# Later W1 regions asked for one by one, and the last block's gates by exponentials and a logarithm with their table loaded by name

## The chip, the cores and the metric

The kernel runs on one core of one Trainium2 chip. The metric is the device time of one execution in microseconds. The core has the engines TensorE (PE, with weight loads as PEld), VectorE (DVE), ScalarE (ACT), GpSimd (POOL) and SyncE (SP), each working through its own instructions in order. Transfers are issued by SP and by ACT in this kernel, and 16 DMA engines carry them out.

## What is computed

Three layers one after the other, all in float32 (cut from the reference):

```python
# attention with 128 random features, 4 batches x 8 heads, 576 positions, head size 64
kv = np.einsum('bhsm,bhsd->bhmd', phi(k), v);  z = np.sum(phi(k), axis=2)
x = (phi(q) @ kv) / (phi(q) . z + 1e-6)          # -> 2304 tokens x 512
# gated layer, 512 -> 1536 -> 512
gate = 1.0 / (1.0 + np.exp(-(x @ w_gate)))
x = gate * (x @ w_val) @ w_out
# soft mixture: 8 experts x 4 slots, F = 1024
logits = x @ phi
d = exp(logits - logits.max(0)); d /= d.sum(0) + 1e-9     # over the tokens
c = exp(logits - logits.max(1)); c /= c.sum(1) + 1e-9     # over the slots
slot_out[e] = np.maximum((d.T @ x)[e] @ w1[e], 0.0) @ w2[e]
return c @ slot_out
```

## The kernel before

All work is first recorded as jobs with a due time and then put into one order by `schedule()`, a list scheduler with costs of its own for each engine, which keeps a time from which an operation may start (`plan.floor`), a due time (`plan.t`) and the tables that ACT has loaded. The order is then issued by one helper line, so that all instructions carry the line L430, and rows are told apart by their tiles. Operations that two engines could do (casts, subtractions) are given to one of them by that scheduler.

The 2304 tokens lie in four blocks of 512 and a last one of 256 (`BLOCKS`). The gated layer walks over them in steps; a step f is one of 12 slices of 128 of the 1536 inner columns, and has three groups of matrix passes on TensorE: ga (x @ w_gate), va (x @ w_val) and o (the product with w_out of the step before). Every float32 operand is split into a rounded upper part and the rest, so that each product takes three passes (`three`); the upper part is a cast on ACT or DVE, the rest a subtraction on POOL or DVE (tiles w, ga_a, gt). Blocks 2 and 3 (`PAIR`) are done together by a scheme of seven products in `pair_jobs`, and the last stretch of it takes the down products of PAIR[0] and then of PAIR[1], twelve slices each. The last block of 256 tokens follows (steps `LAST` to `NS` - 1); then come the mixture's experts.

The weights pass through a ring of six tiles, ws, that SP loads from a scratch tensor wscr in DRAM (`load_part`, 512 KB for two slices or 256 KB for one). The last block's first weight, w0, comes by the first single 256 KB load.

When a block of 512 tokens has its x, the mixture's work on it (`moe2_chunks`) runs beside the next steps: the logits (`chunk_logits`, TensorE tiles `fl<-x2T,phs`), an exponential, four transposes on DVE (`x<-x2T`), and `chunk_back`, which writes the transposed halves back by sixteen moves of 64 KB (`x2T<-x`) on SP. `chunk_slot` uses them.

W1 has eight experts of four pieces of 0.5 MB, W2 as much again. `load_w1` asks for one expert in a region of SBUF that is free by then (`EXTAGS`: XT, XT, g2, g3, g4, XT, g0, g1, where g1 is two halves g1a and g1b) and issues four DMAs on ACT; in the trace they are `XT<-in_w`, `g<-in_w`, `g1a<-in_w` and `g1b<-in_w`. Six of the eight are asked for late, at due times of 32, 24, 16, 8 and 5 us before and 2 us after the planned start of the last block. Those are due times and not bounds: an operation of the stream "ex" may be issued 20 us early by the scheduler's lead. W2's pieces are issued on SP (`more<-in_w`, `gt<-in_w`, `ws<-in_w`). The DMA semaphores are eight, taken in turn by the transfers of SP and ACT together, and an issue waits until the transfer that used its semaphore before has landed.

The gate is a sigmoid. For the steps of blocks 0 and 1 it is exp(min(g, 0) - ln(1 + exp(-|g|))), with the product's PSUM tile ga kept until DVE has read it a second time; for the last block (`LAST <= i < SIGS`) it is one Sigmoid instruction on ACT. Exp and Ln are together in the table "natural_log_exp_and_others", and Sigmoid is in another one; ACT loads a table (ACT_TABLE_LOAD) whenever the next function isn't in the loaded one.

## Time and profile before

| | |
|---|---|
| three runs, us | 676.39, 667.46, 667.24 |
| median, us | 667.46 |
| profiled execution, us (its span) | 673.26 (671.5) |
| busy share of the span: PE, DVE, ACT, POOL | 96%, 74%, 62%, 41% |
| granted TensorE clock, mean | 0.989 |
| HBM traffic over the span | 199 GB/s |
| DMA packets moved | 138.48 MB |

The rows further down come from views of this one profiled execution. A timeline lists what an engine did in order, neighbours of one kind joined with their count; in brackets stands the idle time ahead of it and the instruction that ended it. The chain follows the work that ended last back from the end. Windows give busy time within a stretch. Names stand as output tile <- input tiles.

### The profile page before, as it was taken

The page shows a single profiled execution, that of the slowest core. Times are in us where ns is not written, and L with a number is a line of the kernel's source. Part 1 is how long each engine was busy: PE and PEld are TensorE (multiplying, and loading weights), DVE is VectorE, ACT ScalarE, POOL GpSimd, SP SyncE. Part 2 cuts the span into 40 slices and gives each one's busy share as a digit, 9 for nine tenths or more (in the row PEclk, how much of TensorE's full clock was granted, in tenths as well). Part 3 has the DMA queues.
Part 4 walks back from the last instruction along what each step waited for, and adds up shares of the span by engine and source line. Part 5 has one row for each costly group of instructions (what it writes and reads, how often), then busy time and mean ns, then how long its engine had stood idle before and what let it go on. Part 6 is the DMA issues. An engine that isn't in the chain of part 4 may idle for free.

```text
span 671.5 us, 12766 instructions
## 1 busy us (share of the span) xinstructions
PE 644.8 (96%) x4220; PEld 510.5 (76%) x4220; DVE 494.0 (74%) x1475; ACT 413.9 (62%) x938; POOL 273.9 (41%) x259
## 2 busy tenths in 40 slices
PE   7898999999999999899999999999999979999995
PEld 5675677778888778788877688788888859889564
DVE  5989998999899877779788986646638646756323
ACT  5899888889988867778776263443541326445012
POOL 0544445454544433326335645545542433342100
PEclk9999999999999999999999999999999989999898
DMA  7879566778886655623527442221239988777888
GB/s 250 307 267 300 203 216 211 258 231 282 279 274 228 175 180 190 196 84 111 165 74 248 158 124 68 74 82 32 67 100 331 297 260 303 232 234 266 310 341 243
DMA packets 63857, 138.48 MB, mean 206 GB/s; under 512 B 7216, under 2 KB 21296, under 8 KB 63792
## 3 DMA queue, kind: packets, MB, share of 16 engines
q1 hardware_dynamic: 57968, 120.30, 55.2%
q10 hardware_dynamic: 5824, 17.37, 7.6%
q8 instruction: 33, 0.54, 0.3%
q14 instruction: 32, 0.26, 0.1%
HBM read 116.15 MB, written 17.30 MB: 199 GB/s over the span
## 4 chain that ended last, share of the span: by engine, by line
PE 70%; DMA 10%; DVE 8%; ACT 3%; issue 3%; SPq 2%; POOL 2%; DVEq 0%; POOLq 0%; ACTq 0%
PE o L430 20%; PE fl L430 18%; PE ga L430 16%; PE va L430 16%; DVE g L430 3%; DMA g<-in_tok 3%; SPq L430 2%; DMA qscr<-g 2%; DMA ws<-wscr 1%; DMA g<-in_w 1%; DMA g<-qscr 1%; ACT ga_a L430 1%; DVE XT L430 1%; DVE x2T L430 1%; DMA XT<-in_w 1%
## 5 line engine op out<-in xcount | busy, mean ns | idle before, releaser
L430 POOL TENSOR_TENSOR w<-ws,w 128x512 fp32r<-128x512 f32 (+1 forms) x95 | 113.3, 1193 | 168.9 <-ACT w L430 54.4
L430 PE MATMUL o<-gt,w 128*128 128x512 f32 (+1 forms) x576 | 135.2, 374 | 2.4 <-ACT w L430 1.0
L430 PEld LDWEIGHTS o<-gt,w 128*128 128x128 f32 x576 | 97.9, 190 | 25.2 <-issue 4.1
L430 PE MATMUL ga<-XT,w 128*128 128x512 f32 (+1 forms) x432 | 100.9, 368 | 2.9 <-DVE XT L430 0.9
L430 ACT ACTIVATE w<-ws 128x512 fp32r<-128x512 f32 (+1 forms) x102 | 59.0, 581 | 71.4 <-PE o L430 24.2
L430 PE MATMUL va<-XT,w 128*128 128x512 f32 (+1 forms) x432 | 98.2, 363 | 0.0
L430 ACT ACTIVATE g<-g 128x128 f32<-128x128 f32 (+5 forms) x214 | 78.3, 422 | 17.7 <-DVE g L430 11.6
L430 PE MATMUL fl<-g,g 64*128 64x128 f32 (+4 forms) x686 | 84.3, 315 | 3.5 <-DVE g L430 1.5
L430 PEld LDWEIGHTS ga<-XT,w 128*128 128x128 f32 x432 | 69.9, 189 | 18.8 <-issue 3.0
L430 PEld LDWEIGHTS va<-XT,w 128*128 128x128 f32 x432 | 70.8, 189 | 12.9 <-issue 1.5
L430 PEld LDWEIGHTS fl<-g,g 64*128 64x128 f32 (+2 forms) x686 | 61.1, 185 | 24.0 <-issue 7.9
L430 ACT ACTIVATE x2T<-g 128x512 f32<-128x512 f32 x72 | 46.0, 667 | 5.3 <-DVE x L430 3.5
L430 ACT ACTIVATE g1b<-g1b,g 128x128 f32<-128x128 f32 x128 | 40.5, 389 | 1.2 <-DVE g L430 1.2
L430 PE MATMUL o<-gt,ga_a 128*128 128x512 f32 x144 | 37.2, 405 | 4.2 <-DVE gt L430 3.9
L430 DVE TENSOR_SCALAR x2T<-x2T 128x512 f32<-128x512 f32 (+1 forms) x72 | 36.4, 515 | 1.1 <-ACT x2T L430 1.0
L430 PEld LDWEIGHTS o<-gt,ga_a 128*128 128x128 f32 x144 | 27.3, 194 | 11.2 <-ACT ga_a L430 4.3
L430 DVE TENSOR_TENSOR w<-ws,w 128x512 fp32r<-128x512 f32 (+1 forms) x31 | 22.6, 731 | 17.3 <-ACT w L430 17.1
L430 DVE CUSTOM_DVE_ANT_0 g<-fl,g 128x128 f32<-128x128 f32 x142 | 32.2, 285 | 3.4 <-PE fl L430 3.3
L430 POOL TENSOR_TENSOR g<-g 128x512 f32<-128x512 f32 (+1 forms) x20 | 23.0, 1149 | 28.7 <-DMA g<-in_tok 19.5
L430 DVE TENSOR_TENSOR XT<-fl,XT 128x512 f32<-128x512 f32 x24 | 16.5, 689 | 21.9 <-PE fl L430 21.9
L430 ACT ACTIVATE ga_a<-ga_a 128x512 f32<-128x512 f32 x48 | 29.9, 623 | 3.7 <-DVE ga_a L430 3.4
L430 POOL TENSOR_TENSOR w<-x,w 128x512 fp32r<-128x512 f32 x17 | 21.8, 1284 | 25.3 <-ACT w L430 8.9
(261 smaller groups left out, 1262.9 us busy)
## 6 DMA issues: line engine op xcount, KB each, us to landing
ws<-wscr SPq DMA_DIRECT2D x42, 512.0 KB, 3.9
g<-in_wall SPq DMA_DIRECT2D x36, 512.0 KB, 4.9
ws<-wscr SPq DMA_DIRECT2D x54, 256.0 KB, 3.8
wscr<-x SPq DMA_DIRECT2D x36, 256.0 KB, 4.4
g<-in_qkT SPq DMA_DIRECT2D x15, 576.0 KB, 4.9
g<-in_tok SPq DMA_DIRECT2D x15, 576.0 KB, 5.3
g<-in_w ACTq DMA_DIRECT2D x16, 512.0 KB, 6.5
XT<-in_w ACTq DMA_DIRECT2D x12, 512.0 KB, 4.8
```

The lines of the kernel that those rows point to most:

```text
L430: ins = getattr(self.eng[e], method)(*a, **k)
```

## The change

There are five edits. `SIGS` goes from 99 to 0, so that the last block's twelve gates take the long form: Abs, Exp and Ln on ACT, a scalar_tensor_tensor on DVE that reads ga again, and an Exp on ACT, in the place of one Sigmoid. Ahead of PAIR[0]'s logits' exponential the common table is loaded by name (`preload_act_table_set`), and the scheduler counts it as loading that table. The six late W1 regions keep their due times (written as `W1AT`) but get floors in the planner's time of 480 to 535 (`W1FLOOR`). And `M2A` puts PAIR[0]'s mixture chunks 2 us later on the list.

```diff
--- before.py
+++ after.py
@@ -45,6 +45,7 @@
 
 W_LO = float(np.uint32(0x38000000).view(np.float32))
 BIG = 3.0e38
+EXP_LN = "natural_log_exp_and_others"
 W_HI = float(np.uint32(0x47EFFFFF).view(np.float32))
 
 
@@ -79,9 +80,11 @@
 SPANQ = 147.0
 SPAND = 33.0
 READY = 12.0
-SIGS = 99
+SIGS = 0
+W1AT = (1.0, 9.0, 17.0, 25.0, 28.0, 35.0)
+W1FLOOR = (480,491,502,513,524,535)
 EARLY = 30
-M2A = -32.0
+M2A = -30.0
 M2B = 0.66
 M2C = 3.75
 M2D = 0.7
@@ -399,6 +402,7 @@
                     alt = next(a for a in alts if a[0] == e)
                     c, held = self.cost(e, alt[1], alt[3], outs, ins)
                     want = {AF.Exp: 0, AF.Ln: 0, AF.Sigmoid: 1}.get(alt[3].get("func"), table) if e == "ACT" else table
+                    want = 0 if alt[1].startswith("preload") else want
                     if want != table:
                         c, table = c + RELOAD, want
                     if held:
@@ -1047,6 +1051,8 @@
             DVE.tensor_tensor(out=new, in0=new, in1=mrun[0:p], op=ALU.max)
         DVE.tensor_scalar(out=neg, in0=new, scalar1=-1.0, scalar2=None, op0=ALU.mult)
         DVE.tensor_copy(out=lt[0:p, 1, :], in_=ps)
+        if j == PAIR[0] and SIGS < NS:
+            plan.place([("ACT", "preload_act_table_set", (EXP_LN,), {})], [lt[0:p, 0, :]], [ps, SG[1]])
         ACT.activation(out=lt[0:p, 0, :], in_=ps, func=AF.Exp, bias=neg, accum_out=row)
         if j != DONE[0]:
             ACT.activation(out=old, in_=mrun[0:p], func=AF.Exp, bias=neg)
@@ -1133,13 +1139,15 @@
         t = T([128, 1024 * n], tag, F32, bufs)
         return [t[:, 1024 * c:1024 * c + 1024] for c in range(n)]
 
-    def load_w1():
+    def load_w1(k=None):
 
         e = len(W1)
+        plan.floor = 0.0 if k is None else W1FLOOR[k]
         if e < E:
             W1.append(pieces(EXTAGS[e], 3 if EXTAGS[e] == "XT" else 1))
             for c in range(4):
                 ACT.dma_start(out=W1[e][c], in_=w1[e, :, 1024 * c:1024 * c + 1024])
+        plan.floor = 0.0
 
     def load_w2():
 
@@ -1352,7 +1360,7 @@
                 plan.t -= 5.0 * last
 
     stream("att", T0)
-    ACT.preload_act_table_set("natural_log_exp_and_others")
+    ACT.preload_act_table_set(EXP_LN)
     DVE.memset(g4[:, 0:256], 0.0)
     warm(g4[:, 0:256], W0N, "va")
     for h in range(2):
@@ -1537,10 +1545,10 @@
             m2_jobs(0, start + 3.0, 60.0)
             jobs += [(start + 4.0, "ex", load_w1), (start + 12.0, "ex", load_w1)]
             start = pair_jobs(start)
-            jobs += [(start - SPAND + 1.0 + 8 * k, "ex", load_w1) for k in range(4)]
+            jobs += [(start - SPAND + x, "ex", lambda k=k: load_w1(k)) for k, x in enumerate(W1AT)]
             m2_jobs(PAIR[0], start + M2A, span * M2B)
             m2_jobs(PAIR[1], start + M2C, span * M2D)
-            jobs += [(start - 5.0, "ex", load_w1), (start + 2.0, "ex", load_w1), (start + 8.0, "ex", free_more),
+            jobs += [(start + 8.0, "ex", free_more),
                      (start + span * 0.9, "end", free_halves), (start + span * 0.85, "m2", join_slots)]
         for f in range(f0, f1):
             jobs += moe_jobs(i, start + span * (f - f0) / (f1 - f0), span / (f1 - f0))
```

The programs are the same up to the last down products of PAIR[0]. In full, ACT has 715 rows before and 745 after, DVE 1379 and 1386, PE 839 and 847, SP 247 and 248; table loads are 13 before and 5 after.

SP's order at PAIR[0]'s moves (`x2T<-x_588` before, `x_592` after; `ws<-wscr 128x2x512` is a 512 KB load, 128x512 a single one, of which the first is the last block's first weight). Before:

```order
L430 DMA ws<-wscr 128x2x512 x13
L430 DMA x2T<-x_588 32x512 x4
L430 DMA ws<-wscr 128x2x512
L430 DMA x2T<-x_588 32x512 x7
L430 DMA ws<-wscr 128x2x512
L430 DMA x2T<-x_588 32x512 x5
L430 DMA ws<-wscr 128x512 x9
```

and after:

```order
L434 DMA ws<-wscr 128x2x512 x12
L434 DMA x2T<-x_592 32x512 x2
L434 DMA ws<-wscr 128x2x512
L434 DMA x2T<-x_592 32x512 x7
L434 DMA ws<-wscr 128x2x512
L434 DMA x2T<-x_592 32x512 x7
L434 DMA ws<-wscr 128x2x512
L434 DMA ws<-wscr 128x512 x4
```

One 512 KB load has moved from ahead of the sixteen moves to behind the first two; the single loads follow the last of the three 512 KB loads.

DVE's order around the four transposes (`STREAM_TRANSPOSE`) that feed these moves. Before:

```order
L430 COPY x2T<-o_513 128x512
L430 COPY x2T<-o_515 128x512
L430 CAST ga_a<-ws 128x512
L430 CAST gt<-g_493 128x512
L430 TENSOR_TENSOR gt<-g_493,gt 128x512
L430 STREAM_TRANSPOSE x_588<-x2T 128x512
L430 CAST gt<-g_493 128x512
L430 STREAM_TRANSPOSE x_588<-x2T 128x512
L430 TENSOR_TENSOR gt<-g_493,gt 128x512
L430 TENSOR_REDUCE mx_582<-fl 128x1
L430 COPY lt<-fl 128x128
L430 TENSOR_TENSOR mx_582<-mx_582,mrun 128x1
```

and after:

```order
L434 CAST gt<-g_493 128x512
L434 CAST w_574<-ws 128x512
L434 TENSOR_TENSOR gt<-g_493,gt 128x512
L434 CAST gt<-g_493 128x512
L434 TENSOR_TENSOR gt<-g_493,gt 128x512
L434 STREAM_TRANSPOSE x_592<-x2T 128x512 x3
L434 CAST gt<-g_493 128x512
L434 STREAM_TRANSPOSE x_592<-x2T 128x512
L434 TENSOR_TENSOR gt<-g_493,gt 128x512
L434 TENSOR_REDUCE mx_587<-fl 128x1
L434 COPY lt<-fl 128x128
```

Two copies of x2T are no longer DVE's, and three transposes stand together, ahead of the logits' maximum (`TENSOR_REDUCE mx`).

ACT's order from PAIR[0]'s x2T copies up to the first single weights (`in_w` rows are W1 pieces of 0.5 MB). Before:

```order
L430 DMA g_598<-in_w 128x1024
L430 ACTIVATE w_589<-ws 128x512
L430 DMA g_609<-in_w 128x1024 x2
L430 ACTIVATE ga_a<-ws 128x512
L430 DMA g_609<-in_w 128x1024
L430 ACT_TABLE_LOAD
L430 ACTIVATE lt,mx_582<-fl,mx_582 128x128
L430 DMA g_609<-in_w 128x1024
L430 ACTIVATE mx_582<-mrun,mx_582 128x1
L430 ACTIVATE cs<-cs 128x128
L430 ACTIVATE ga_a<-ws 128x512
L430 DMA XT<-in_w 128x1024
```

and after:

```order
L434 DMA g_594<-in_w 128x1024 x2
L434 ACT_TABLE_LOAD
L434 ACTIVATE lt,mx_587<-fl,mx_587 128x128
L434 ACTIVATE mx_587<-mrun,mx_587 128x1
L434 DMA g_594<-in_w 128x1024
L434 ACTIVATE ga_a<-ws 128x512
L434 ACTIVATE cs<-cs 128x128
L434 DMA g_594<-in_w 128x1024
L434 ACTIVATE w_605<-ws 128x512
L434 DMA g_609<-in_w 128x1024 x2
L434 ACTIVATE w_611<-ws 128x512
L434 DMA g_609<-in_w 128x1024
```

The four x2T copies stand together on ACT just above this place after the change. By the row of the table load 13 W1 pieces have gone out before, counted from the first half of g1b, and 6 after. Between the last x2T copy on ACT and the last block's first weight (w_617 in both) stand 8 pieces before and 7 after.

ACT's order at the last block's first gates. Before:

```order
L430 ACT_TABLE_LOAD
L430 ACTIVATE ga_a<-ga 128x256
L430 ACTIVATE w_632<-ws 128x512
L430 DMA g_624<-in_w 128x1024
L430 ACTIVATE gt<-ga_a 128x256
L430 ACTIVATE ga_a<-ga 128x256
L430 ACTIVATE w_641<-ws 128x512
L430 DMA g1a<-in_w 128x1024
L430 ACTIVATE w_643<-ws 128x512
L430 ACTIVATE w_648<-ws 128x512
L430 ACTIVATE ga_a<-ga 128x256
```

and after:

```order
L434 ACTIVATE ga_a<-ga 128x256
L434 ACTIVATE ga_a<-ga_a 128x256
L434 ACTIVATE ga_a<-ga_a,one_b 128x256
L434 ACTIVATE w_632<-ws 128x512
L434 DMA XT<-in_w 128x1024
L434 ACTIVATE ga_a<-ga_a 128x256
L434 DMA XT<-in_w 128x1024
L434 ACTIVATE ga_a<-ga 128x256
L434 ACTIVATE w_641<-ws 128x512
L434 ACTIVATE ga_a<-ga_a 128x256
L434 ACTIVATE lt,mx_638<-fl,mx_638 128x128
L434 ACTIVATE ga_a<-ga_a,one_b 128x256
```

The table load and the Sigmoid (`ga_a<-ga`) of each gate have become Abs (`ga_a<-ga`), Exp (`ga_a<-ga_a`), Ln (`ga_a<-ga_a,one_b`) and Exp, with a weight cast or a W1 piece between them. Of the 24 late W1 pieces 3 stand behind the first gate before, and 10 after.

## Rows read from the trace of the kernel before

**Rows 1.** windows: busy us (instructions) of PE, PEld, DVE, ACT, POOL; PEclk, DMA share, GB/s
```profile
540.00:545.00 5.00, 1.07 (x5) 0.46 (x3) 1.70 (x4) 1.15 (x2) 0.56 (x1) 0.96 0.60 166
545.00:550.00 5.00, 4.72 (x16) 3.41 (x15) 4.13 (x6) 1.78 (x3) 2.54 (x3) 0.70 1.00 358
553.00:616.00 63.00, 60.60 (x500) 57.18 (x497) 41.23 (x89) 31.42 (x52) 26.06 (x20) 1.00 0.77 250
```

**Rows 2.** PE timeline of quiet steps: start, us, engine, operation, tiles, count
```profile
594.98 1.60 PE L430 MATMUL ga<-XT,w 128*128 128x256 f32 x12
...
599.30 1.60 PE L430 MATMUL ga<-XT,w 128*128 128x256 f32 x12
```

**Rows 3.** PE timeline around stall A, idle before and its releaser in brackets
```profile
537.63 2.88 PE L430 MATMUL o<-gt,w 128*128 128x512 f32 x12
544.44 1.49 PE L430 MATMUL o<-gt,ga_a 128*128 128x512 f32 x3 [3.92 <-DVE gt L430]
546.20 3.15 PE L430 MATMUL o<-gt,ga_a 128*128 128x512 f32 x9 [0.28 <-POOL ga_a L430]
549.19 1.07 PE L430 MATMUL o<-gt,w 128*128 128x512 f32 x4
```

**Rows 4.** chain that ended last: start, us, what
```profile
508.85 8.16 PE o L430 x36
...
537.87 4.71 DMA ws<-wscr
...
542.60 0.64 ACT w L430
...
543.26 0.69 DVE w L430
```

**Rows 5.** SP timeline: the x2T moves of block 0, then of PAIR[0]
```profile
391.63 2.41 SPq L430 DMA_DIRECT2D x2T<-x  x4
...
400.71 3.04 SPq L430 DMA_DIRECT2D x2T<-x  x5
...
522.17 4.22 SPq L430 DMA_DIRECT2D x2T<-x  x4
...
533.08 4.70 SPq L430 DMA_DIRECT2D x2T<-x  x5
```

**Rows 6.** DMA issues, KB each, median us to landing: 388 to 406, then 519 to 541
```profile
x2T<-x SPq DMA_DIRECT2D x16, 64.0 KB, 3.4
...
x2T<-x SPq DMA_DIRECT2D x16, 64.0 KB, 5.3
```

**Rows 7.** PE timeline around stall B
```profile
582.73 0.38 PE L430 MATMUL o<-gt,w 128*128 128x256 f32 x1 [0.97 <-ACT w L430]
583.79 1.57 PE L430 MATMUL o<-gt,w 128*128 128x256 f32 x11 [0.68 <-DVE gt L430]
...
589.37 1.46 PE L430 MATMUL o<-gt,w 128*128 128x256 f32 x10 [0.75 <-POOL w L430]
```

**Rows 8.** ACT timeline at stall B
```profile
582.05 0.63 ACT L430 ACTIVATE w<-ws 128x512 fp32r<-128x512 f32 x1 [5.40 <-DMA ws<-wscr]
```

**Rows 9.** ACT groups by form: total us, mean ns; table loads from 516 us on
```profile
L430 ACT ACT_TABLE_LOAD x9 | 11.5, 1283 | 0.2
L430 ACT ACTIVATE ga_a<-ga 128x256 f32<-128x256 f32 x12 | 4.6, 380 | 5.5 <-PE ga L430 5.4
...
L430 ACT ACTIVATE g<-g 128x256 f32<-128x256 f32 x1 | 0.4, 416 | 2.3 <-DMA g<-in_tok 2.3
...
L430 ACT ACTIVATE g<-fl,den_b 128x288 f32<-128x288 f32 x11 | 5.4, 488 | 1.0 <-PE fl L430 1.0
```

**Rows 10.** DVE groups by form, whole run
```profile
L430 DVE SCALAR_TENSOR_TENSOR ga_a<-ga,maske,ga_a 128x256 f32<-128x256 f32 x3 | 1.5, 485 | 3.7 <-PE ga L430 3.7
```

**Rows 11.** ACT timeline in the tail
```profile
618.72 1.28 ACT L430 ACT_TABLE_LOAD   x1
620.01 0.26 ACT L430 ACTIVATE dt<-dt 128x64 f32<-128x64 f32 x1
```

## Prediction

> **What bounds the kernel now.** I read the windows first, to see where TensorE is not full, then TensorE's timeline around each gap, and then the chain of work that ended last, backwards from the gap. In the windows of the stretch that the change touches, TensorE is short of work in two places [rows 1]: from 540 to 550 us it is busy for 1.07 and 4.72 of 5 us, with a granted clock of 0.70 in the second window, and from 553 to 616 it is busy for 60.60 of 63, the lack being around 582 to 590. Elsewhere the last block's steps run without a gap: a step is twelve passes each of ga, va and o, and from one step's ga to the next is 4.32 us, 1.44 for each twelve [rows 2].
>
> Stall A [rows 3]: the passes of f=8 start at 537.63, and twelve such passes take 2.72 us (a run of 36 took 8.16 [rows 4]), so f=9 could start at 540.35. It starts at 544.44: 4.09 us late. Its twelve passes then last until 549.19, 4.75 us instead of 2.72; 0.28 of this excess of 2.03 is a second wait, for POOL's ga_a, the rest is the lower clock. Together 6.1 us. The chain [rows 4] says what is late: the single ws load (512 columns, the first weight of the last block) was issued at 537.87, landed after 4.71 us, ACT cast it at 542.60, DVE subtracted at 543.26, and only then came the gt that TensorE waits for. ACT executes in order, so f=9's ga_a cast stood behind that first weight, and all of it behind one DMA. Why was it issued so late? The SP queue [rows 5]: sixteen x2T moves and two 512 KB ws loads stand ahead of it, from 522.17 to 537.78, 15.6 us. The same sixteen moves and two loads for block 0, when no W1 load is about, ran from 391.63 to 403.75, 12.1 us, and a move landed in 3.4 us instead of 5.3 [rows 6].
>
> Stall B [rows 7]: idle 0.97, 0.68 and 0.75 us at 582.73, 583.79 and 589.37, 2.4 us. ACT had waited 5.40 us for a ws load when it cast the weight that ended the first of them [rows 8]; PAIR[1]'s sixteen x2T moves sit between the ws loads on SP there.
>
> So 8.5 us can be won in this part of the program. The profiled execution is 671.5 us in span (673.26 in all), the median of three runs 667.46, 0.994 of the span; sums are made in the span and scaled by that.
>
> **The change, part by part.** *Table loads.* Nine from 516 us on become one (the named one ahead of the logits' Exp stands where the first of the nine is now): 8 x 1.283 = 10.3 us of ACT go [rows 9]. *Gates.* In each of twelve steps the Sigmoid (0.380) becomes an Abs of the same tile, taken at 0.38, and Exp, Ln and Exp, which the trace has for other widths: Exp on 128x256 in SBUF once at 0.416, Ln at 288 columns 0.488; so 0.42 + 0.49 + 0.42 = 1.33 us, x12 = 16.0 us. ACT gains 5.7 us net. DVE gains twelve scalar_tensor_tensor from PSUM at 0.485 = 5.8 us [rows 10]. The last block's 63 us have ACT at 31.4 and DVE at 41.2 us busy [rows 1], so both have room: about 37 and 47 of 63. Neither lies on TensorE's path as busy time; what counts is latency. The ga bank now comes free after Abs 0.38, one weight cast of 0.64 between [rows 4], Exp 0.42, Ln 0.49, DVE 0.49: 2.42 us after ga's last pass, and TensorE writes ga again 2.88 us after it (va and o, 1.44 each) [rows 2]. About 0.4 us to spare with the hand-offs still to pay. The gt of a step is wanted 5.76 us after ga's end (four passes of 1.44) and would be ready at about 4.3. Price nothing; cover gone (one ACT instruction held for over 0.4 us), each microsecond more is a microsecond on the end.
>
> *W1's loads.* 24 loads of 0.5 MB are issued by ACT from 500 us on. By the orders, 21 of them stand ahead of the last block's first gate now and 14 after the change; 3 and 10 behind it. Between the last x2T copy on ACT and the first weight of the last block, the stretch of stall A, 8 stand now and 7 after: barely lighter. What is lighter is the backlog before it.
>
> *SP.* One 512 KB ws load moves behind the first two moves, so the single ws load now has sixteen moves and three loads ahead of it. DVE has two x2T copies less, and does three of the four transposes together, ahead of the logits' reductions that stood between them. The first move is issued at 522.17 now, and I put it 2.3 us earlier, at about 519.8; this is my estimate from the order (two copies and three reduction rows fewer ahead of the last transpose), with no row for it. From there the single ws goes out after 12.1 + 0.6 us at best (block 0's rate) and 15.6 + 0.6 at worst: 532.5 to 536.0. It lands 4.71 us later, and f=9 starts 1.86 us behind that, as now (542.58 to 544.44): 539.1 to 542.6, against 540.35 needed. So the wait of 4.09 becomes 0 to 2.2. With seven W1 loads still in the stretch I go nearer the worst: start at 541.8, wait 1.5, 2.6 won. Of the 2.03 behind it I take half, 1.0, as the pause before it is shorter. Bounds of stall A: 1.9 to 6.1 won, taken 3.6.
>
> *Stall B.* PAIR[1]'s moves should start some 2 us earlier with the rest, which could spare all 2.4 us; but seven more W1 loads now run among the last block's ws loads, which could cost the same again at other steps. Bounds 2.4 won and 2.4 lost (more is the second rival); I take 0.4 won.
>
> *The rest.* M2A's 2 us move the logits between TensorE passes that have no gap: nothing. One table load less in the tail, at 618.72 [rows 11], could bring its own 1.28 us at most; taken as nothing, since TensorE has passes of its own there. Weight casts that change from ACT to DVE: nothing, as both have idle time in the stretch.
>
> Sum: 671.5 − 3.6 − 0.4 = 667.5, times 0.994 = 663.5 us.
>
> On the table loads the Trainium skill, page "ScalarE: Activation LUTs", section "What ACT_TABLE_LOAD costs", counts 1283 ns and a drain of about 1380 ns for each switch; by that the eight loads would be 21.3 us of ACT and ACT would gain no busy time but lose 5. Here a load is 1.28 us and the next activation starts right behind it [rows 11], so the drain isn't seen, and the sum goes by 10.3.
>
> **The rivals.**
> 1. *Both stalls go whole.* If the moves run at block 0's rate, A costs nothing, and the last block's W1 loads fit: −8.5, 663.0 in span, 659. For it: the best bound 539.1 is ahead of 540.35. Against: seven W1 loads stay in the stretch, and B has its own cause.
> 2. *The W1 loads on ACT hold the gates: slower.* Ten loads now stand in ACT's order between gate instructions. The DMA semaphores are shared by ACT and SP in turn, and an issue waits when the transfer eight before it hasn't landed: between 522 and 538 such waits stretched SP's sixteen moves by 3.5 us [rows 5]. If each of the seven added loads holds ACT by 1.5 us, that is 1.1 over the spare 0.4, x7 = 7.7; less the 2.6 to 3.6 won at A, +4 to +5: 675.5 in span, 672. It decides from about 0.9 us held a load on. For it: the DMA engines' share is already 0.77 over the last block [rows 1], and ACT idled 5.40 us for one ws load there [rows 8]. Against: the seven are spread over some 40 us, and ACT had 31.6 of 63 us free.
> 3. *Stall A isn't W1's.* If the sixteen moves take 15.6 us at whatever load, and the ws that now stands behind them takes 4.71 or more, A shrinks by the 1.7 us of the earlier start and B grows by as much: within 1 us of 667.5 in the median.
>
> A rule of the Trainium skill speaks for the second rival: page "DMA: Bandwidth & Descriptors", section "Issuing engines are not separate DMA queues": transfers of all issuing engines share the 16 DMA engines and interleave. By it nothing is relieved where W1's seven loads stay beside the moves, and the last block's ws loads pay for the other seven. The trace agrees that they share: a move landed in 3.4 us without W1's loads and in 5.3 with them [rows 6].
>
> **How the numbers follow.** The likeliest, 0.45: both shortened, 661 to 666, predicted 663.5. Both gone 0.15 (659). Stall A not W1's 0.15 (667). Slower 0.25 (669 to 674). The range, 657 to 673, reaches 2 us below the first rival, since the shorter runs without a profile may not have the stalls at the profile's size, and to the second's price with a little over it; it leaves out some two in ten, at both ends. What a measurement of this kernel can tell from no change is about 2%, 13.3 us: faster than 654.1 would need more than the 8.5 us that can be won, 0.03; slower than 680.8 would need rival 2 at twice its price, 0.05; within, 0.92.
>
> **What would show it.** Right: TensorE's idle before f=9 (the o passes on gt and ga_a) under 2.2 us; the single ws load issued before 536; the clock in the window behind it above 0.70; table loads from 516 us on down to one; ACT's busy share of the last block about 37 of 63 us. Wrong: TensorE waiting on a ga pass for DVE or on an o pass for a gt in steps 1 to 8 of the last block, with ACT idle before it for a DMA; f=9 starting later than 544.4; or ws loads of the last block landing after more than 6 us.

## The result and the profile after

The changed kernel is slower. Over twenty runs each, its median is 674.86 us (670.55 to 679.74) and that of the kernel before 669.62 us; the ratio is 1.0077, with a 95% interval of 1.0055 to 1.0099. The prediction was 663.5 us with a range up to 673.0: the wrong side, and outside the range. It was made against a median of three runs of 667.46 us; twenty runs put the kernel before 2.2 us higher, but as a ratio the forecast was 0.994, so that doesn't rescue it. Medians and ratios, here and below, leave out runs more than 1.5% above the fastest of the same kernel (one of six in e4, one of ten in e8, three of twelve in e12, none elsewhere). A ratio is the one on record, over runs of the same session, and not the quotient of the two medians shown.

| | before | after |
|---|---|---|
| median of 20 runs, us | 669.62 | 674.86 |
| span of the profiled execution, us | 671.5 | 674.6 |
| mean granted clock of TensorE | 0.989 | 0.985 |
| ACT busy in the last block | 31.42 of 63.00 us | 36.69 of 69.90 us |
| table loads in the whole program | 13 | 5 |

TensorE's timeline of the kernel after, first around the old stall A and then in the last block; the columns are start, duration, operation, tiles and count, and in brackets the idle time ahead and what ended it:

```profile
540.67 0.47 PE L434 MATMUL o<-gt,ga_a 128*128 128x512 f32 x1 [3.16 <-DVE gt L434]
541.52 0.79 PE L434 MATMUL o<-gt,ga_a 128*128 128x512 f32 x2 [0.37 <-DVE gt L434]
542.98 4.21 PE L434 MATMUL o<-gt,ga_a 128*128 128x512 f32 x9 [0.67 <-POOL ga_a L434]
546.98 3.36 PE L434 MATMUL o<-gt,w 128*128 128x512 f32 x10
```

```profile
578.42 1.70 PE L434 MATMUL ga<-XT,w 128*128 128x256 f32 x12 [1.05 <-DVE ga_a L434]
...
588.44 2.93 PE L434 MATMUL ga<-XT,w 128*128 128x256 f32 x12 [3.75 <-DVE ga_a L434]
591.17 2.52 PE L434 MATMUL va<-XT,w 128*128 128x256 f32 x12
...
606.48 1.70 PE L434 MATMUL va<-XT,w 128*128 128x256 f32 x12 [0.87 <-DVE ga_a L434]
...
620.05 1.66 PE L434 MATMUL o<-gt,w 128*128 128x256 f32 x12 [0.75 <-DVE gt L434]
```

Stall A is still there: idle 3.16, 0.37 and 0.67 us, 4.20 in all, exactly the sum of [rows 3]. The two groups behind it, starting at 540.67 and 546.98, then take 6.31 us (with the two shorter waits) and 3.75 us, where the kernel before took 4.75 and 2.81 and a group without a stall takes 2.72. Where the kernel before waited in the last block for weights, 2.4 us in all [rows 7], the kernel after waits at ga and va for DVE's ga_a, the gate: 1.05, 3.75 and 0.87 us, and 0.75 for a gt at its end; with 0.30 for a weight that is 6.7 us. Behind the longest of these a group of twelve passes takes 2.73 us (588.44 to 591.17) instead of 1.44.

Windows of the kernel after, for the stretches that answer to [rows 1] (columns as there):

```profile
540.00:545.00 5.00, 3.28 (x8) 2.12 (x9) 4.07 (x7) 0.51 (x1) 2.08 (x2) 0.71 0.90 274
545.00:550.00 5.00, 5.00 (x16) 3.91 (x15) 1.63 (x3) 0.63 (x1) 0.48 (x1) 0.61 0.77 227
551.70:621.60 69.90, 62.94 (x502) 59.34 (x498) 41.18 (x100) 36.69 (x83) 28.13 (x21) 0.95 0.79 262
585.00:590.00 5.00, 1.56 (x7) 1.56 (x8) 2.94 (x11) 0.71 (x2) 2.29 (x2) 0.64 1.02 393
590.00:595.00 5.00, 5.00 (x32) 5.00 (x32) 1.56 (x6) 2.65 (x6) 1.28 (x1) 0.67 0.66 240
```

The lower clock lasts two windows after stall A (0.71, 0.61) where it lasted one before (0.70), and the kernel before has no such window in the last block, where this one has two (0.64, 0.67). Part of that is chance: a second profile of the kernel before (e5, further down) has 0.50 and 0.94 after stall A, and one window of 0.68 in the last block.

Profiles of two executions can't be laid over each other by their times: the kernel after reaches the same point of the program 3.7 us earlier, and the second profile of the kernel before reaches it 4.4 us earlier, by chance of what lies ahead. A point behind which the orders begin to differ is the group of twelve o passes that starts at 511.40 us before and at 507.69 after. Measured from there, the kernel after is later by 0.0 us at the start of f=9, 2.5 at the first gate, 3.7 at the ga of step 5, 8.2 at that of step 8, 8.9 at the first passes of the tail (`ga<-x2T,phs`), and 6.8 at the end. So 2.5 us are lost around stall A, 6.5 in the last block (69.9 us from its first gate to the tail, 63.4 before), and 2.1 come back in the tail. Of the 6.5 us, 4.3 are more idle time of TensorE (6.7 for 2.4); the rest is mostly the passes at the lower clock.

Why the last block loses: ACT and DVE of the kernel after around its longest stall, and the chain of work that ended last there.

```profile
576.43 0.63 ACT L434 ACTIVATE w<-ws 128x512 fp32r<-128x512 f32 x1 [1.52 <-DMA ws<-wscr]
...
579.71 0.33 ACTq L434 DMA_DIRECT2D g<-in_w  x1
...
580.34 0.33 ACTq L434 DMA_DIRECT2D g<-in_w  x1
...
580.73 0.43 ACTq L434 DMA_DIRECT2D g1a<-in_w  x1
...
588.42 0.42 ACT L434 ACTIVATE ga_a<-ga_a 128x256 f32<-128x256 f32 x1 [6.46 <-DVE ga_a L434]
```

```profile
583.67 0.43 DVE L434 CAST w<-ws 128x512 fp32r<-128x512 f32 x1 [3.34 <-DMA ws<-wscr]
...
586.97 0.43 DVE L434 CAST w<-ws 128x512 fp32r<-128x512 f32 x1 [2.07 <-DMA ws<-wscr]
...
587.97 0.42 DVE L434 SCALAR_TENSOR_TENSOR ga_a<-ga,ga_a 128x256 f32<-128x256 f32 x1
```

```profile
580.07 6.77 DMA ws<-wscr
...
588.05 0.34 DVE ga_a L434
...
588.44 2.93 PE ga L434 x12
```

The gate's Exp at 588.42 waits 6.46 us for DVE; DVE's second reading of ga at 587.97 stands behind two weight casts that wait 3.34 and 2.07 us for their ws loads; and the chain names the ws load, issued at 580.07 and landing after 6.77 us. Three W1 pieces of 0.5 MB were issued beside it, at 579.71, 580.34 and 580.73, SP had put a W2 piece ahead of it at 579.17, and the window behind them (585 to 590) moves 393 GB/s. So this stall has two parts, a late ws load and a gate that stands behind it in an in-order queue. The experiments take them apart.

### The profile page after: what moved, and what is told of

Its sections match the earlier page's. It is cut to its first block, busy times and chain, and to the rows that moved or that the text cites. A ratio compares the mean times of both kernels' runs of the same rounds, so it can differ in the third digit from the quotient of the medians.

```text
span 674.6 us, 12781 instructions
## 1 busy us (share of the span) xinstructions
PE 644.3 (96%) x4220; PEld 511.6 (76%) x4220; DVE 490.6 (73%) x1485; ACT 416.8 (62%) x967; POOL 273.9 (41%) x260
## 4 chain that ended last, share of the span: by engine, by line
PE 70%; DMA 11%; DVE 9%; ACT 4%; issue 2%; SPq 2%; POOL 1%; DVEq 0%; POOLq 0%; ACTq 0%
PE o L434 20%; PE fl L434 19%; PE ga L434 16%; PE va L434 16%; DMA ws<-wscr 4%; DVE g L434 4%; DMA g<-in_tok 2%; DMA qscr<-g 2%; SPq L434 2%; ACT ga_a L434 1%; DMA g<-qscr 1%; DMA x2T<-x 1%; DVE ga_a L434 1%; DMA g<-in_w 1%; DVE x2T L434 1%
## 5 line engine op out<-in xcount | busy, mean ns | idle before, releaser
L434 POOL TENSOR_TENSOR w<-ws,w 128x512 fp32r<-128x512 f32 (+1 forms) x96 | 115.3, 1202 | 177.0 <-ACT w L434 48.1
L434 ACT ACTIVATE g<-g 128x128 f32<-128x128 f32 (+5 forms) x214 | 78.1, 422 | 15.4 <-DVE g L434 10.6
L434 ACT ACTIVATE ga_a<-ga_a 128x512 f32<-128x512 f32 (+1 forms) x72 | 39.7, 552 | 12.3 <-DVE ga_a L434 11.9
L434 ACT ACTIVATE ga_a<-ga 128x512 f32<-128x512 f32 (+1 forms) x36 | 18.8, 522 | 21.7 <-PE ga L434 21.5
```

The source lines that it names most:

```text
L434: ins = getattr(self.eng[e], method)(*a, **k)
```

## The experiments

Each kernel is the kernel before or after with the edit shown. Two readings are given: the ratio to the kernel before, and, from the profile, by how much it is later (+) or earlier (−) than the kernel before, counted from the common point. Step 5 and step 8 are the ga of that step, and can be off by about 1 us, since passes of the mixture stand ahead of them in one order and behind them in another; "tail" is the first pass behind the last block, where all of them are through.

| us, minus before | f=9 | first gate | step 5 | step 8 | tail | end | ratio |
|---|---|---|---|---|---|---|---|
| before, second profile (e5) | −0.6 | 0.7 | 0.7 | 2.2 | 2.2 | 2.2 | 1 |
| after | 0.0 | 2.5 | 3.7 | 8.2 | 8.9 | 6.8 | 1.0077 |
| gates only (e1) | 5.7 | 3.9 | 6.3 | 4.0 | 4.2 | 2.0 | 1.0033 |
| floors only (e2) | 0.6 | 1.6 | 2.1 | 6.7 | 8.2 | 6.4 | 1.0096 |
| after without floors (e3) | 0.9 | 2.2 | 5.0 | 1.5 | 1.7 | −0.5 | 1.0033 |
| after, gate that reads ga once (e4) | −1.8 | −0.4 | 0.6 | 7.9 | 10.6 | 8.4 | 1.0178 |
| after, W1 to a quarter (e6) | −3.4 | −4.9 | −4.9 | −4.6 | −5.4 | −7.1 | 0.9914 |
| before, W1 to a quarter (e7) | −4.1 | −5.0 | −5.0 | −6.9 | −6.9 | −8.5 | 0.986 |
| floors only, W1 to a quarter (e13) | −3.5 | −5.0 | −4.6 | −7.0 | −5.7 | −7.4 | 0.9874 |
| before, join_slots earlier (e9) | 1.7 | 1.7 | 1.7 | 0.4 | 0.4 | −1.3 | 1.0009 |
| after, last floors later (e10) | −1.6 | −0.1 | −0.5 | −1.4 | 2.1 | −0.1 | 1.0025 |
| both held back (e14) | −3.9 | −3.4 | −3.4 | −1.0 | 0.9 | −1.0 | 0.9969 |
| the same with Sigmoid (e15) | −4.1 | −3.2 | −3.7 | −3.1 | −0.9 | −0.9 | 1.0017 |

The second profile of the kernel before shows how far two executions of one program differ by themselves: 2.2 us at the end. Single runs of it, told by their whole times, differ by up to 10 us (666.45 to 676.39), so that a difference of 2 us between two profiles shows nothing by itself.

### Gates or floors: e1, e2, e3

e1 is the kernel after with M2A and the six W1 regions as before:

```diff
-M2A = -30.0
+M2A = -32.0
...
-            jobs += [(start - SPAND + x, "ex", lambda k=k: load_w1(k)) for k, x in enumerate(W1AT)]
+            jobs += [(start - SPAND + 1.0 + 8 * k, "ex", load_w1) for k in range(4)]
...
-            jobs += [(start + 8.0, "ex", free_more),
+            jobs += [(start - 5.0, "ex", load_w1), (start + 2.0, "ex", load_w1), (start + 8.0, "ex", free_more),
```

> Of the change only the gates and the table loaded by name; the six W1 regions and M2A as before. Theory A (the long gate is the cause: its Exp and the scalar_tensor_tensor that frees ga stand behind weight casts that wait for a ws load, and TensorE waits at ga): slower than before by 2 to 5 us, ratio 1.003 to 1.0075, with idle time of TensorE at ga passes ended by DVE's ga_a of over 2 us. Theory B (the W1 pieces moved into the last block make its ws loads late, and the gates cost nothing by themselves): within 1 us of before, ratio 0.9985 to 1.0015, and no idle time at ga passes.

Measured: 671.98 us, ratio 1.0033 (1.0010 to 1.0055). TensorE's timeline of it:

```profile
539.72 0.79 PE L434 MATMUL o<-gt,w 128*128 128x512 f32 x1 [6.10 <-DVE gt L434]
541.18 4.63 PE L434 MATMUL o<-gt,w 128*128 128x512 f32 x10 [0.67 <-POOL w L434]
...
580.18 1.69 PE L434 MATMUL ga<-XT,w 128*128 128x256 f32 x12 [1.95 <-DVE ga_a L434]
```

Theory A's size and sign hold at their lower edge, and a wait of 1.95 us at a ga pass for DVE's ga_a is there (0.39 at another). But the profile is later than before by 3.9 us at the first gate already, where no long gate has run yet, because stall A came out larger (6.10 and 0.67 us idle); the last block itself, where the gates run, takes 63.7 us, against 63.4 and 64.9 in the two profiles of the kernel before. So the slowdown of e1 is not seen where theory A has it.

e2 keeps the floors alone:

```diff
-SIGS = 0
+SIGS = 99
...
-M2A = -30.0
+M2A = -32.0
```

> Of the change only the floors of the six W1 regions; Sigmoid gates and M2A as before. Theory A: within 1.5 us of before, ratio 0.997 to 1.002, since a Sigmoid frees ga in one instruction. Theory B: slower by 3 to 5 us, ratio 1.0045 to 1.0075, TensorE waiting in the last block for weights (o passes ended by ACT or POOL w).

Measured: 677.11 us, ratio 1.0096 (1.0063 to 1.0129): theory B's sign, and more than its size. TensorE's longest wait in the last block and the piece of the chain ahead of it:

```profile
582.13 0.80 PE L434 MATMUL va<-XT,w 128*128 128x256 f32 x2 [3.83 <-ACT w L434]
```

```profile
573.88 7.46 DMA ws<-wscr
```

The Sigmoid kernel waits too, and as long (3.83 us): here for the weight itself, whose ws load took 7.46 us. So floors alone give the whole slowdown, as far as two overlapping intervals tell, and the gates don't add to it: the last block takes 69.95 us here and 69.90 in the kernel after. Both kernels wait for a late ws load; with the long gate the gate stands behind the weight cast and TensorE stops at ga, with the Sigmoid it stops at the pass that needs the weight.

e3 is the kernel after with the regions asked for as before, so e1 with M2A at −30:

```diff
-            jobs += [(start - SPAND + x, "ex", lambda k=k: load_w1(k)) for k, x in enumerate(W1AT)]
+            jobs += [(start - SPAND + 1.0 + 8 * k, "ex", load_w1) for k in range(4)]
...
-            jobs += [(start + 8.0, "ex", free_more),
+            jobs += [(start - 5.0, "ex", load_w1), (start + 2.0, "ex", load_w1), (start + 8.0, "ex", free_more),
```

> The changed kernel with the six W1 regions asked for as before; gates and M2A stay changed. Theory A: slower than before by 2 to 5 us, like the gates alone. Theory B: within 1 us of before. If M2A is a cause of its own, this run stands apart from the gates alone by over 2 us.

Measured: 671.88 us, ratio 1.0033 (1.0007 to 1.0058), as e1: M2A is no cause of its own. Its last block takes 62.9 us, no more than before. By the ratios of the three runs, the floors cost about 6.4 us alone, the gates and their table about 2.2 (the interval of e1 runs from 0.7 to 3.7), and together they cost 5.2.

### A gate that reads ga once: e4

```diff
+        if i >= LAST:
+            ACT.activation(out=a, in_=ps, func=AF.Exp, scale=-1.0)
+            DVE.tensor_scalar(out=a, in0=a, scalar1=1.0, scalar2=None, op0=ALU.add)
+            DVE.reciprocal(out=a, in_=a)
+            return a
```

> The changed kernel, but the last block's gate is 1/(1+exp(-ga)): one Exp on ACT that reads ga once, then an addition of 1 and a reciprocal on DVE in SBUF, with the same table. ga is free after one ACT instruction, as with the Sigmoid. Theory A: 4 to 7 us faster than the changed kernel, at or below before (ratio 0.993 to 1.001), no idle time over 0.5 us at ga passes. Theory B: 0 to 2 us faster than the changed kernel, ratio 1.005 to 1.008, as the ws loads are as late as before.

Measured: 682.33 us, ratio 1.0178 (1.0149 to 1.0207), slower than either theory allowed. A reciprocal of 128x256 is dear, and twelve of them put 20.9 us on DVE; but DVE is busy for 53.6 of the 74.5 us of the last block, and TensorE's longest wait there is another one:

```profile
L434 DVE RECIPROCAL ga_a<-ga_a 128x256 f32<-128x256 f32 x12 | 20.9, 1742 | 0.1
```

```profile
584.19 1.89 PE L434 MATMUL fl<-x2T,dt 128*32 128x512 f32 x2 [5.93 <-DMA ws<-wscr]
```

TensorE waits 5.93 us for a transfer, ahead of passes of the mixture that read what the sixteen x2T moves bring; the profile names a ws load, and the last of these moves landed at 583.74 us. It is between steps 5 and 8 that this kernel loses 7.3 us. Its waits for the gate's ga_a come to 0.4 us in all, as theory A expected of a gate that frees ga at once, and the time that theory A promised for that isn't won. So the run speaks for late transfers. How much of the slowdown is the reciprocal's own isn't shown.

### The kernel before a second time: e5

> The kernel before, unchanged, for a second profile of it. If stall A (4.2 us of idle time at f=9), stall B (2.4 us) and the lower clock from 620 to 630 us belong to its order, all three are seen again, each within 1 us (clock 0.81 and 0.85, within 0.05); what is not seen again is chance of one execution, and a difference between two profiles of that size says nothing.

Stall A (3.30 us) and B (3.21) are there again, each within the 1 us that was expected; B is 0.8 us longer and at one place instead of three. A lower clock in the tail is there again too, but not at its size: 0.66 and 1.00 in the two windows, for 0.81 and 0.85.

```profile
539.43 5.97 PE L430 MATMUL o<-gt,ga_a 128*128 128x512 f32 x12 [3.30 <-DVE gt L430]
...
578.29 1.46 PE L430 MATMUL ga<-XT,w 128*128 128x256 f32 x10 [3.21 <-DVE w L430]
```

```profile
620.00:625.00 5.00, 4.98 (x55) 2.71 (x58) 1.72 (x8) 0.26 (x1) 0.95 (x1) 0.66 0.58 197
625.00:630.00 5.00, 5.00 (x93) 2.66 (x89) 1.59 (x6) 0.00 (x0) 0.95 (x1) 1.00 0.92 288
```

### W1's pieces cut to a quarter: e6, e7, e13

Each late piece moves 128 KB. The diff shows what is run; the cut is made when the instruction is issued, behind the planner, which still counts the whole piece, so that the order of instructions stays the same on every queue:

```diff
-                ACT.dma_start(out=W1[e][c], in_=w1[e, :, 1024 * c:1024 * c + 1024])
+                ACT.dma_start(out=W1[e][c][:, 0:256], in_=w1[e, :, 1024 * c:1024 * c + 256])
...
-                PE.matmul(ps[32 * g:32 * g + 32, :], si[:, k, :], W1[e][k][:, 256 * g:256 * g + 256],
+                PE.matmul(ps[32 * g:32 * g + 32, :], si[:, k, :], W1[e][k][:, 0:256],
```

(for e of 2 and over). On the kernel after:

> The changed kernel in the same order, but each of the 24 late W1 pieces is loaded to a quarter (128 KB, its first 256 columns, which then stand for all four in the expert's first product). Theory B (the bytes of W1's pieces make the ws loads late): TensorE's idle time before the last block's first gate and in its steps, 10.2 us in the changed kernel, falls under 2 us, and the time to about 660 to 664 us. Theory C (ws loads are late because of their place on SP behind the x2T moves, whatever W1 loads): idle time stays over 6 us, the time over 669.

On the kernel before:

> The kernel before in the same order, with the 24 late W1 pieces cut to a quarter in the same way. Theory B: idle time of stalls A and B, 6.6 us before, under 1.5 us, the time about 661 us. Theory C: A stays over 3 us, the time over 666.

On the floors alone, run later:

> The floors alone (Sigmoid gates, M2A as before) with the 24 late W1 pieces cut to a quarter, beside the changed kernel cut in the same way (665.0 us; it has 3.3 us of idle time left, 2.2 of it at a ga pass and an o pass that wait for the long gate). If the long gates cost by themselves: 2 to 3 us faster than that, about 662, as the kernel before cut in the same way (661.9), with no idle time at ga passes. If they don't: within 1 us of 665.

Measured: 664.99 us, ratio 0.9914 (0.9878 to 0.9950), for the kernel after; 661.93 us, 0.9860 (0.9786 to 0.9934), for the one before; 662.22 us, 0.9874 (0.9836 to 0.9912), for the floors alone. TensorE's two longest waits between 500 and 612 us in the kernel after with a quarter of the bytes, both on the gates' way; the floors alone have none over 0.25 us there:

```profile
581.65 1.70 PE L446 MATMUL ga<-XT,w 128*128 128x256 f32 x12 [1.49 <-DVE ga_a L446]
...
609.64 1.67 PE L446 MATMUL o<-gt,w 128*128 128x256 f32 x12 [0.75 <-DVE gt L446]
```

In e7, SP's moves and the ws load behind them (the first move, the load, and from the chain its landing) are these:

```profile
519.42 2.42 SPq L442 DMA_DIRECT2D x2T<-x  x4
...
530.86 13.43 SPq L442 DMA_DIRECT2D ws<-wscr  x8
```

```profile
530.86 4.55 DMA ws<-wscr
```

From the first move to the first weight's load are 11.4 us, where the kernel before took 15.7 (522.17 to 537.87), and the load lands after 4.55 us instead of 4.71: with fewer bytes of W1 about, the same row of issues is through 4.3 us earlier. Theory B holds and theory C falls: with the same instructions in the same places on every queue, stall A goes when W1's bytes go (0.58 us left in e7, none in e6 and e13), and of stall B 0.91 us of 2.40 is left in e7. The kernel after keeps 2.8 us of idle time in its last block, more than the 2 us expected, and is 1 us above the expected time; 2.2 of it is at the two passes above, which wait for the gate. The bytes cost the kernel before 1.4% of its time and the floors-only kernel 2.2% (1.0096 less 0.9874); with a quarter of them the floors cost nothing that can be seen. So the floors are slow only through what their pieces do to other loads. For the kernel after the times say less: with a quarter of the bytes it is 3.1 us above the kernel before by the medians (5.2 with all of them), in intervals that overlap, as e7 has two runs. By the profiles, the 8.9 us that it is later at the tail become 1.5. The difference of e6 and e13, 2.8 us in the medians, would be what the long gates (and M2A) cost there by themselves; it is of the size of e1's 2.2, but e13 has two runs, and in the profiles the two end within 0.3 us of each other and their last blocks take 62.9 and 62.7 us.

### The last pieces behind the moves: e10

```diff
-W1FLOOR = (480,491,502,513,524,535)
+W1FLOOR = (480, 491, 502, 513, 552, 558)
```

> The changed kernel with two of its six floors moved: 524 and 535 become 552 and 558, so that the last eight pieces go out behind the last block's sixteen x2T moves instead of among the ws loads at 579 to 581. Theory B (pieces among the last block's ws loads are what costs): the stall at ga near 588, 3.75 us and the lower clock behind it, is gone, 4 to 6 us faster than the changed kernel, ratio to before 0.999 to 1.002; the part ahead of the first gate stays 2 to 3 us behind before. Rival: the experts' first products wait for the late pieces near 635 to 645, and the time is that of the changed kernel or more.

Measured: 670.28 us, ratio 1.0025 (0.9990 to 1.0060), 0.5% or 3.5 us faster than the kernel after by the ratios, whose intervals just touch; 4 to 6 were expected. No wait at a ga pass is left in its profile; the longest ones in the last block are these:

```profile
594.95 0.63 PE L434 MATMUL fl<-dt,acc 128*128 128x32 f32 x4 [1.21 <-DVE acc L434]
...
611.48 1.67 PE L434 MATMUL o<-gt,w 128*128 128x256 f32 x12 [1.54 <-DVE gt L434]
```

Its profile loses nothing ahead of the first gate (−0.1), where 2 to 3 us were expected, although the edit changes nothing there: the size of stall A varies between executions. From the first gate to the tail it loses 2.1 us, the kernel after 6.5, and no window of its last block from 575 us on has a lower clock. The rival didn't come: TensorE waits for no W1 piece in the tail.

### Weights and narrow passes elsewhere: e8, e9

e8 holds w0's cast back on the kernel before:

```diff
-        add(t + SPAND - 6.0, lambda: (split_w(LAST, 0), split_w(LAST, 1)))
+        def first_two():
+            plan.floor = 510.5
+            split_w(LAST, 0)
+            split_w(LAST, 1)
+            plan.floor = 0.0
+
+        add(t + SPAND - 6.0, first_two)
```

> The kernel before with one edit: the first two weights of the last block may not be cast before 510.5 us of the planner's time, which puts w0's cast on ACT and its subtraction on DVE behind f=9's own. If stall A is one late weight standing in front of work that doesn't need it, A falls from 4.2 us of idle time to under 1 us and the kernel is 4 to 6 us faster (ratio 0.991 to 0.994). If f=9's own loads are as late as w0's, A stays over 3 us and the time within 1 us of before; if the stall only moves to the first gate, idle time appears there.

Measured: 668.43 us, ratio 0.9970 (0.9939 to 1.0001). That is between both expectations, and the interval reaches no change. The profile is of an execution of 675.61 us and isn't read here. That this one weight is the whole of stall A isn't borne out (4 to 6 us faster were expected of that, and 2.0 came by the ratio); that it is a part isn't shown.

e9 moves join_slots on the kernel before. By its new place it is recorded ahead of PAIR[1]'s last accumulation, so that this part is missing from the slots; the same instructions run. That holds for e11 and e12 as well.

```diff
-                     (start + span * 0.9, "end", free_halves), (start + span * 0.85, "m2", join_slots)]
+                     (start + span * 0.9, "end", free_halves), (start + span * 0.7, "m2", join_slots)]
```

> The kernel before with one number changed: join_slots (passes fl<-dt,acc and fl<-srep,lt) due at 0.70 of the last block instead of 0.85. In both profiles of the kernel before these narrow passes stand 3.7 us ahead of the tail and the clock is 0.66 to 0.85 from 620 to 630; in the kernels where they stand over 7 us ahead it stays at 1.00. If their place is the cause, the clock in the tail is 1.00 and the kernel 1.5 to 2.5 us faster (ratio 0.996 to 0.998). If not, the lower clock is still seen, and the time within 1 us of before.

Measured: 669.43 us, ratio 1.0009 (0.9983 to 1.0034). The clock in the tail is at its full level, where e5 had 0.66:

```profile
620.00:625.00 5.00, 4.98 (x81) 3.50 (x84) 1.90 (x9) 0.26 (x1) 1.85 (x2) 1.00 1.01 392
```

and the tail takes 53.4 us instead of 55.1. But stall A was larger in this execution (5.32 us idle), and the median shows no gain. Nor does the place alone decide over the clock: e7 has the passes of join_slots where the kernel before has them, 3.70 us ahead of the tail, and its clock is at its full level in every window from 595 to 635 us, as here:

```profile
610.00:615.00 5.00, 4.84 (x59) 3.93 (x62) 2.02 (x8) 1.01 (x4) 0.91 (x1) 1.00 0.90 335
```

(e7; its tail begins at 606.79.)

### A version to beat both: e11, e12, e14, e15

e11 and e12 put the findings together: M2A at −32, e8's edit, e9's edit, and

```diff
-W1FLOOR = (480,491,502,513,524,535)
+W1FLOOR = (0, 0, 0, 514, 552, 558)
```

> A version meant to be faster than both: the changed kernel's gates with their table, M2A as before, w0's cast behind f=9's, join_slots at 0.70, and the floors 0, 0, 0, 514, 552, 558, so that eight pieces go out as their regions come free, the next four only after w0, and the last eight behind the x2T moves of PAIR[1]. Theory B: stall A under 2 us, stall B under 1.5 us, no lower clock in the tail; 5 to 8 us faster than before, ratio 0.988 to 0.993. Theory A (the long gates cost 2 us by themselves) would have it 2 us slower than the same with Sigmoid.

> The same version with the Sigmoid gates and their table loads as before. Theory B: 5 to 8 us faster than before, ratio 0.988 to 0.993, within 1.5 us of the same with the long gates. Theory A: 2 us faster than that one.

Measured: 668.83 us, ratio 0.9997 (0.9962 to 1.0031), with the gates, and 673.31 us, 1.0081 (1.0041 to 1.0120), with the Sigmoid. Both miss. TensorE's timeline and the chain of e11 show stall A at its old size:

```profile
542.39 4.44 PE L434 MATMUL o<-gt,ga_a 128*128 128x512 f32 x11 [5.50 <-DVE gt L434]
```

```profile
534.94 6.28 DMA ws<-wscr
```

The ws load at 534.94 took 6.28 us with W1 held back (its nearest piece went out at 536.78), but SP had put two W2 pieces of 0.5 MB right ahead of it and behind it, at 534.38 and 535.36. And e12, whose last W1 piece goes out at 617.3 us, 7 us into the tail (ahead of the tail in e11), waits in it:

```profile
640.67 0.64 PE L434 MATMUL o<-g,XT 128*32 128x128 f32 x16 [0.64 <-DMA g<-in_w]
641.93 0.65 PE L434 MATMUL o<-g,XT 128*32 128x128 f32 x16 [0.62 <-DMA g<-in_w]
```

These waits are for W2's pieces, by their tiles in regions that W1 had before, and the tail takes 59.4 us instead of 55.1; that the late W1 piece is the cause isn't shown. e14 and e15 therefore hold W2's first pieces back too, and put join_slots at 0.85 again:

```diff
-W1FLOOR = (0, 0, 0, 514, 552, 558)
+W1FLOOR = (0, 0, 0, 514, 535, 548)
...
-        plan.floor = plan.t
+        plan.floor = 543.0
         load_w2()
```

> e11 with join_slots back at 0.85 (the whole computation), W2's first pieces held back by a floor of 543, and W1's floors 0, 0, 0, 514, 535, 548; the long gates. If any 0.5 MB piece in front of a ws load does it: stall A under 2 us (5.5 in e11), the last block's idle time under 2.5 us, 4 to 7 us faster than before, ratio 0.990 to 0.994. If stall A has another cause it stays over 4 us and the ratio is 0.997 or more.

> The same with Sigmoid gates and their table loads. If the long gates cost 2 us by themselves: 1 to 3 us faster than e14, ratio 0.986 to 0.991. If not, within 1 us of e14; if the tail waits for W2's later pieces as in e12, slower than before.

Measured: e14 668.43 us, ratio 0.9969 (0.9947 to 0.9992); e15 671.69 us, 1.0017 (0.9991 to 1.0044). TensorE's waits around f=9 and the longest in the last block of e14:

```profile
539.51 3.17 PE L434 MATMUL o<-gt,ga_a 128*128 128x512 f32 x11 [0.81 <-DVE gt L434]
...
544.34 2.12 PE L434 MATMUL o<-gt,w 128*128 128x512 f32 x8 [0.62 <-POOL w L434]
...
587.33 0.74 PE L434 MATMUL o<-gt,w 128*128 128x256 f32 x4 [0.80 <-ACT w L434]
```

Stall A is 0.81 and 0.62 us, as expected where no 0.5 MB piece stands in front of a ws load, and the kernel is 3.4 us ahead at the first gate; it gives all of that back in the last block (67.7 us for 63.4), where W1's and W2's pieces now are. e14 is faster than both kernels, by 2.1 us or 0.3% than the one before, which is half of the least that was expected. e15, the same with Sigmoid gates, is slower than e14 by 3.3 us in the medians, against the 1 to 3 us faster that the long gate's own price would have given. In the profiles the two end within 0.1 us of each other: e15's last block is 2.0 us shorter (65.8), and its tail 1.9 us longer (55.0 for 53.1), with a clock of 0.82 and 0.84 in two windows of it.

## Why the prediction was wrong

**What bounds the kernel, and where.** Right. The two stalls are in both profiles of the kernel before (4.2 and 2.4 us, then 3.30 and 3.21), and e7 shows that they were there to be won: with a quarter of W1's bytes the kernel takes 661.9 us, 8.5 less. That this is the sum that the prediction gave for both stalls is in part luck: by e7's profile 5.0 us of it are ahead of the first gate (6.1 in the sum), 1.9 in the last block (2.4) and 1.7 in the tail, of which the sum had nothing. The prediction's account of why the load went out late is borne out by e7 too (11.4 us for the row of moves, 12.1 at block 0, 15.6 in the kernel before).

**Table loads and gates.** Right in their sums: eight loads went, the added operations measured 409, 508 and 419 ns for 0.42, 0.49 and 0.49 us, and ACT is busy for 36.7 us in the last block (now 69.9 us long) for 37 expected.

```profile
L434 ACT ACTIVATE ga_a<-ga_a 128x256 f32<-128x256 f32 x24 | 9.8, 409 | 8.2 <-DVE ga_a L434 8.1
...
L434 ACT ACT_TABLE_LOAD x5 | 6.4, 1283 | 1.0 <-PEq L1647 0.7 <-issue 0.2
...
L434 ACT ACTIVATE ga_a<-ga_a,one_b 128x256 f32<-128x256 f32 x12 | 6.1, 508 | 0.3
```

**The price of the gates.** The step "Price nothing", with about 0.4 us to spare, was right only where every ws load is on time. The condition that the step named, an ACT instruction held over 0.4 us, is what happens at 576.43, where a weight cast between a gate's Abs and its Exp waits 1.52 us, and the ga behind it comes 1.05 us late. And one term was left out: behind the last step there are no further passes to cover its gate. Every profile with long gates has TensorE wait at the last o passes for DVE's gt (0.75 us after, 0.29 in e1 and e3, 0.75 in e6, 1.54 in e10, 0.47 in e11, 0.76 in e14), and none with the Sigmoid does.

**Stall A.** The step's queue was right and its landing was not. The first x2T move was issued at 515.58 in the kernel after, 519.3 by the clock of before, for 519.8 estimated; the ws load that f=9 waits for went out at about 532.0, which is 535.7, inside 532.5 to 536.0:

```profile
515.58 1.15 SPq L434 DMA_DIRECT2D x2T<-x  x2
...
530.59 9.95 SPq L434 DMA_DIRECT2D ws<-wscr  x5
```

But the prediction let it land after 4.71 us as before, and it took 6.80 (532.01 to 538.81), with three W1 pieces on their way that ACT had issued from 526.98 to 530.00 (two) and at 532.19, and the other ws loads beside it. The rows are two from ACT's timeline and one from the chain (W1's regions go by the tile name g):

```profile
526.98 3.02 ACTq L434 DMA_DIRECT2D g<-in_w  x2
...
532.19 0.34 ACTq L434 DMA_DIRECT2D g<-in_w  x1
```

```profile
532.19 6.64 DMA g<-in_w
```

The chain names the last W1 piece, since it landed 0.01 us behind the ws load (538.83); the cast at 538.84 reads the ws tile. In e6, with the same order and a quarter of the bytes, the same load landed after 4.82 us.

The 1.86 us from the landing to f=9 held (538.81 to 540.67). With 6.80 in the place of 4.71 the step's own chain gives 544.4, the start measured. The second half, 1.0 us won from a shorter pause, turned into 1.6 lost at f=9's own passes and 0.9 at the next twelve, as the pause was no shorter and the clock stayed low for two groups instead of one. So 3.6 us won became 2.5 lost.

**Stall B.** The term that failed most: 0.4 us won, with 2.4 as the bound of the loss. The sentence beside it had the cause ("seven more W1 loads now run among the last block's ws loads") and took the size from the stalls that the trace of before happened to have there. The last block took 6.5 us more than before.

**The rivals.** The second had the sign, the place and nearly the size (+4 to +5 us; 5.2 measured), and was given 0.25. Its mechanism was only half right: the gates are held in ACT's and DVE's order, but by weight casts that wait for ws loads; the W1 issues that it blamed went out without holding ACT at the long stall (0.33 to 0.43 us each at 579.71, 580.34 and 580.73). The sentence of the Trainium skill, page "DMA: Bandwidth & Descriptors", section "Issuing engines are not separate DMA queues", which was set beside it, was the better guide: transfers of all issuers run on the same 16 DMA engines and interleave. e6, e7 and e13 agree with it: the same issues with a quarter of the bytes remove stall A and most of the waits behind it. The prediction had itself concluded from it that nothing is relieved where other loads still run, and gave that 0.25. The third rival, that stall A is not W1's, is refuted by e7.

**The weights of the cases.** 0.45 went to the case that both stalls shrink, although the order of after showed 7 pieces for 8 in the stretch of stall A and ten for three behind the first gate. Read together these two counts say that no stretch with ws loads was emptied and one was filled.

What stays open: the size of the gates' own price. It is 2.2 us by the ratios of e1 and of e3, and 2.8 in e6 against e13, while with full W1 and floors the gates are not slower than the Sigmoid (1.0077 and 1.0096, intervals that overlap), and in e14 against e15 they are faster. In the stretch where they run, the last block, the profiles give next to nothing for three pairs (63.7 and 62.9 us against 63.4 and 64.9; 69.9 against 70.0; 62.9 against 62.7) and 2.0 us for one (67.7 against 65.8), and e1's and e3's loss stands ahead of the first gate, where no long gate has run. A late ws load that either kernel has to wait for would hide a price, and e2's stall fits that; each edit also gives another order, so that a difference of 2 us between two orders can't be put down to one part.

## What to carry to other kernels

A transfer that is not urgent is not free: before it is moved to a later stretch, list the loads that are urgent there, and price each one at the landing time that the trace shows in a crowded stretch, not at that of the load it replaces. A chain of several instructions on in-order engines has the slack of its slowest neighbour: look what stands between its parts, and what those wait for. And to find out whether bytes or places in a queue cost, keep the order and cut the bytes.

## What the hardware showed beside that

DVE's reciprocal of 128x256 took 1742 ns (e4) where a scalar_tensor_tensor of that size took 419. And TensorE's clock fell in the tail of some kernels though TensorE was busy for over 4.8 of the 5 us in each of these windows: 0.81 and 0.85 before, 0.66 in e5, 0.82 and 0.84 in e15. It costs about 2 us: the tail takes 55.0 to 55.1 us in these three profiles and 52.8 to 53.5 in the others that are read here (e12 aside, with its waits), and this is what the kernel after got back in its tail. In the three, the narrow passes of join_slots begin 3.4 to 3.7 us ahead of the tail's first passes, and in the others over 7 us ahead, with one exception that keeps the cause open: e7, with the order of the kernel before and 3.7 us, ran at the full clock. The run that moved the join alone (e9) shows the clock, and no gain in its median.
